# Turning the gathered rows of a routed expert layer's slots, and a block of the layer behind it, on VectorE and through DRAM instead of on TensorE

## The chip, the cores and the metric

One core of a Trainium2 chip runs the whole program. The metric is the time of one execution on the device in microseconds (us). PE is TensorE (PEld its weight loads), DVE is VectorE, ACT is ScalarE, POOL is GpSimd, SP is SyncE; a name like SPq stands for the queue of instructions of that engine.

## The reference

Three stages follow one another on 2304 tokens (4 sequences of 576):

```python
attn_out = _attn_ref(q, k, v, f)                       # causal, with decay; 8 heads of 64
x = attn_out.transpose(0, 2, 1, 3).reshape(2304, 512)

logits = x @ w_gate + modality_bias[modality_id]       # 8 experts
e_idx = np.argmax(logits, axis=1)
gate_w = probs[np.arange(N), e_idx]                    # probs: softmax of logits
for e in range(E):
    mask = e_idx == e
    h = np.maximum(x[mask] @ w1[e], 0.0)               # 512 -> 1024
    out[mask] = gate_w[mask, None] * (h @ w2[e])       # 1024 -> 512

h = out @ w_in                                         # 512 -> 2048
g = np.maximum(0.01 * h, h)
return (g @ w_out).astype(np.float32)                  # 2048 -> 512
```

Each token goes through one expert, and then all tokens through the second layer.

## The kernel before, in words

Matrix products of 32-bit numbers are taken as three products of a high and a low part: ACT casts a value to its high part (names that end in h), DVE subtracts it from the value (names that end in l), and PE multiplies high by high, high by low and low by high.

**Slots.** While attention runs, the tokens are sorted by expert into slots of 128 rows. 18 slots (0 to 17) are always computed; as many more follow as the data need, each behind a test (`go`, L1321). With this data there are 20: slots 0 to 19. The expert, and with it both weight matrices, changes at slots 4, 5 and 10 and nowhere else after slot 0.

A slot's rows are gathered from `xs` by an indirect DMA on POOL's queue (L166) into one of two buffers `xg`, whose last column is the gate. PE turns them, four `tx` transposes of 128x128 (L210) into PSUM, and ACT and DVE make `xh` and `xl` of them (L211, L212). `gemm1` (L222, 24 matmuls of 128x512) gives `h`; `keep` is its relu into `hs` on ACT (L227). `trh` (L1119) turns `hs` on PE, eight transposes, with `hh` and `hl` behind them (L1121, L1122). `gemm2` (L1127, 24 matmuls) sums into `yp`. `yout` scales `yp` with the gate column, which `keepg` has copied to `gc` (L1112), into `ys` on ACT (L1133), and POOL scatters `ys` to the rows of `yd` (L1135). The `ys` buffers are two, in turn.

**A step.** `step(t)` (L1165) lays three slots over one another: gemm1 of slot t, trh and gemm2 of slot t-1, and the turn (`trx`) of slot t+1. Between them stand `split`, which makes the high and low parts of the next slot's weights, w1 (L173, L177) or w2, in pairs, each inside an If that is only taken where the expert changes (L189), and `aside`, small pieces on ACT, DVE and POOL that prepare the second layer's weights or compute slot numbers. The whole runs inside `ordered`: on every engine the instructions stand in the order in which the code emits them, and none overtakes another. So the order of lines in `step` is the order of each queue.

From step 3 on, trx of slot t+1 stands after half of gemm2 and after the first w2 splits:

```python
if t:
    gemm2(t - 1, 0, 4)
...
if t:
    split(t, 1, 0)
    split(t, 1, 1)
if nx and TX <= t < NSTAT - 1:
    trx(t + 1, pmx, "tx")
```

**The end.** After the last slot `tail` (L1142) does the last trh and gemm2. Inside it the first block of the second layer is turned. That layer works on five blocks of up to 512 tokens: block b's rows come from `yd` (`xload`, L994) and are turned by `xts` into `fxh` and `fxl`. Blocks 0 and 1 come in four row DMAs each and are turned by PE, 16 `fx` transposes a block (L1034, L1037, L1038); blocks 2 to 4 come by DMAs that put columns in 32 partitions each and are turned in 32x32 blocks by DVE into `xq` (L1022), with cast and subtraction behind (L1025, L1026). Then `g1` (`u`, L1358) and `g2` (`a`, L1378) follow for 16 pieces of the inner width.

Of the kernel before, what the change touches and what calls it, by code (L numbers as in the profile page):

```python
# [9 lines left out]
F32 = mybir.dt.float32  # L10
# [19 lines left out]
XW = DM + 1  # L30
# [8 lines left out]
NFIX = NTOK % FT  # L39
FIX = NTOK - NFIX  # L40
K1 = 4
T1 = 2
N2 = NS - K1
NSET = 6
SIDE = 2
SP = 2.0
TE = 3
TX = 3
PST = 3
MS = ['PE', 'Activation', 'DVE', 'Pool', 'SP']  # L50
MS2 = ['PE', 'Activation', 'DVE', 'Pool', 'SP']
# [25 lines left out]
def fused(ctx: ExitStack, tc, qk0, qk2, vp, f, mid, wg, mb, w1, w2, w_in, w_out, out):  # L77
# [6 lines left out]
    xs = dr.tile([NTOK, XW], F32, name="xs")  # L84
    agd = dr.tile([4, BH, S], F32, name="agd")
    yd = dr.tile([NTOK, XW], F32, name="yd")


    ident = cp.tile([P, P], F32, name="ident")
# [114 lines left out]
    def flags(i, n):  # L204
        WD.append(nc.values_load(nb[0:1, i:i + 1], engines=(mybir.EngineType.Activation, mybir.EngineType.DVE), min_val=0, max_val=2 ** n - 1))

    def trx(t, pool, tag):
        ps = pool.tile([P, 512], F32, tag=tag, name=f"tx{t}")
        for k in range(NKB):
            nc.tensor.transpose(ps[:, k * P:(k + 1) * P], xg[t % 2][:, k * P:(k + 1) * P], ident)  # L210
        nc.scalar.copy(xh[t % 2], ps)  # L211
        nc.vector.tensor_sub(xl[t % 2], ps, xh[t % 2].bitcast(F32))  # L212
# [12 lines left out]
    def keep(t):  # L225
        hp = Hp.pop(t)
        nc.scalar.activation(WL["hs"], hp.rearrange("p a b -> p (a b)"), AF.Relu)  # L227
# [766 lines left out]
    def xload(b):  # L994
        t0, n = blocks[b]
        r = xp.tile([P, FT // P, XW], F32, tag="xr", name=f"xr{b}")
        if b > 1:
            XR[b] = r.rearrange("p c d -> p (c d)")[:, :4 * n]
            for j in range(4):
                nc.sync.dma_start(XR[b][32 * j:32 * j + 32].rearrange("b (q c) -> b q c", c=P), yd[t0:t0 + n, j * P:(j + 1) * P].rearrange("(q b) c -> b q c", b=32))  # L1000
            if t0 < FIX:
                nc.sync.dma_start(tid[:, t0 // P:(t0 + n) // P].unsqueeze(2), yd[t0:t0 + n, DM:].bitcast(I32).rearrange("(c p) o -> p c o", p=P))
            return
        for i in range(n // P):
            XR[b, i] = r[:, i]
            nc.sync.dma_start(XR[b, i], yd[t0 + i * P:t0 + (i + 1) * P, :])
# [6 lines left out]
    def xts(b, sb, psums, part=None):  # L1013
        t0, n = blocks[b]
        if b not in X:
            xtile(b, sb)
        xh, xl = X[b]
        for i in range(n // P) if part is None else part:
            c = slice(i * P, (i + 1) * P)
            if b > 1:  # L1020
                t = XQ[0].tile([P, 512], F32, tag="xq", name=f"xq{b}_{i}")
                tc.keep_in_program_order(nc.vector.transpose(t.rearrange("p (i k c) -> p i k c", i=4, k=NKB), XR[b][:, i * 512:(i + 1) * 512].rearrange("p (i c k) -> p i k c", i=4, k=NKB)))  # L1022
                t = t.rearrange("p (i k c) -> p k i c", i=4, c=32)
                h, l = (x[:, :, c].rearrange("p k (i c) -> p k i c", c=32) for x in (xh, xl))
                tc.keep_in_program_order(nc.scalar.copy(h, t))  # L1025
                tc.keep_in_program_order(nc.vector.tensor_sub(l, t, h.bitcast(F32)))  # L1026
                continue
            r = XR[b, i]
            nc.gpsimd.tensor_copy(tid[:, t0 // P + i:t0 // P + i + 1], r[:, DM:].bitcast(I32))
            rk = r[:, :DM].rearrange("p (c k) -> p k c", k=NKB)  # L1030
            pool, tag = psums[i % len(psums)]
            ps = pool.tile([P, 512], F32, tag=tag, name=f"fx{b}_{i}")
            for k in range(NKB):
                nc.tensor.transpose(ps[:, k * P:(k + 1) * P], rk[:, k], ident)  # L1034
            yield
            ps = ps.rearrange("p (k c) -> p k c", c=P)
# [54 lines left out]
    with tc.tile_pool(name="rt2", reuse_waits="tile", bufs=1) as rt2, \  # L1091
# [10 lines left out]
        w2l = [mw.tile([P, 2, DM], F32R, name=f"w2l{k}") for k in range(4)]  # L1102
        WL["2h"], WL["2l"] = w2h, w2l
        ysc = []
        hh = mw.tile([P, FF], F32R, name="hh")
        hl = mw.tile([P, FF], F32R, name="hl")
        gc = mw.tile([P, 2], F32, name="gc")

        yp = pmy.tile([P, 512], F32, name="yp")

        def keepg(t):
            nc.scalar.copy(gc[:, t % 2:t % 2 + 1], xg[t % 2][:, DM:DM + 1])  # L1112

        def trh(t):
            for n in range(2):
# [5 lines left out]
                nc.scalar.copy(hh[:, c], ps)  # L1121
                nc.vector.tensor_sub(hl[:, c], ps, hh[:, c].bitcast(F32))  # L1122

        def gemm2(t, k0, k1):
            for k in range(k0, k1):
                for i, (ap, wp) in enumerate(((hh, w2h), (hh, w2l), (hl, w2h))):
                    nc.tensor.matmul(yp, lhsT=ap[:, k * P:(k + 1) * P], rhs=wp[k // 2][:, k % 2, :], start=(k == 0 and i == 0), stop=(k == NFB - 1 and i == 2))  # L1127

        def yout(t):
            m, i = at_slot(oidx, t)  # L1130
            o = m[:, i, :]
            ys = m2.tile([P, XW], F32, tag="ys", name=f"ys{t}")
            nc.scalar.mul(ys[:, :DM], yp, gc[:, t % 2:t % 2 + 1])  # L1133
            nc.gpsimd.tensor_copy(ys[:, DM:].bitcast(I32), o[:, 1:2])
            i = nc.gpsimd.indirect_dma_start(out=yd[:, :], out_offset=bass.IndirectOffsetOnAxis(ap=o[:, 0:1], axis=0), in_=ys, in_offset=None, bounds_check=NTOK - 1, oob_is_err=False)  # L1135
            for o_ in ysc:
                tc.declare_no_dep(i.ins, o_.ins, reason="each token has its own row")
            ysc.append(i)

        LATE = NSTAT - 1  # L1140

        def tail(t):  # L1142
            with ordered(tc, MS4):
                if t >= LATE:
                    yout(t - 1)
                trh(t)
                ps = [(pmx, "tx"), (pma, "h"), (pmb, "h"), (pm0, "th")]
                xs_ = [xts(0, xp0, [p], [i]) for i, p in enumerate(ps)]
                for x in xs_[:3]:
                    next(x)  # L1150
                next(xs_[0])
# [13 lines left out]
        def step(t):  # L1165
            nx = t + 1 < NS
            if t > LATE:
                yout(t - 2)
            if not t:
                with tc.issue_after(st["late"].ins):  # L1170
                    split(t, 1, 0)
                    split(t, 1, 1)
            if t == K1 - 1:
                flags(1, N2)
            keepg(t)
            if t > LATE:
                split(t, 0, 3)
            if t + 2 < NS and t + 2 != K1:
                gather(t + 2)
            if t:  # L1180
                gemm1(t, 0, 2, (pma, pmb)[t % 2], "h")
            aside(t, "load")
            if 0 < t < TE:
                trh(t - 1)
            if nx:
                split(t + 1, 0, 0)
            aside(t, "a1")
            aside(t, "a2")
# [12 lines left out]
            if t:
                gemm1(t, 3, 4, (pma, pmb)[t % 2], "h")
                keep(t)
            if t > NSTAT:
                split(t - 1, 1, 3)
            if nx and t >= NSTAT:
                split(t + 1, 0, 2)
            if nx and 0 < t < LATE:
                split(t + 1, 0, 3)
            if t:  # L1210
                gemm2(t - 1, 0, 4)
            if nx and (0 < t < TX or t >= NSTAT - 1):
                trx(t + 1, pmx, "tx")
            if t:
                split(t, 1, 0)
                split(t, 1, 1)
            if nx and TX <= t < NSTAT - 1:
                trx(t + 1, pmx, "tx")
            if t == K1:
                next(fini, 0)  # L1220
            aside(t, "d")
            if t:
                gemm2(t - 1, 4, 8)
            if t < NSTAT:
                split(t, 1, 2)
            if 0 < t < LATE:
                yout(t - 1)
            if t < NSTAT:
                split(t, 1, 3)

        def finish():
            cnt, full, used = runb, early["full"], early["used"]
# [101 lines left out]
    with tc.tile_pool(name="fx", reuse_waits="tile", bufs=1) as fx, \  # L1334
# [5 lines left out]
         tc.tile_pool(name="pfu", reuse_waits="tile", bufs=3, space=PSUM) as pfu:  # L1340
        for i in range(GS, NSET):
            wset(fx, i)
        XQ.append(xq)
        G = {}
        A = {}
        Y = {}
# [137 lines left out]
```

## Time and profile before

| | |
|---|---|
| time, median of 3 runs | 857.75 us (857.01 to 859.49) |
| the profiled execution, its own time | 857.52 us |
| its span in the trace | 855.8 us |
| granted clock of TensorE, mean | 1.00 |
| PE busy | 847.4 us |
| DVE, ACT, POOL busy | 479.0, 403.4, 133.2 us |
| chain that ended last, by engine | PE 94%, DMA 2%, ACT 2%, DVE 1% |

The span is what the trace covers; the execution's own time is 1.7 us longer. Busy time says how long an engine worked, and not whether it was late for anybody. Matmuls overlap one another, so the time that one costs is the distance between two starts. The chain that ended last is followed from the last instruction back to whatever released each one.

### The profile page before, as it was taken

How to read it: one execution, taken by the hardware profiler on the slowest of the kernel's cores; microseconds unless marked ns; L12 is line 12 of the kernel's file. 1: busy time of each engine (PE TensorE's matmuls, PEld its weight loads, DVE VectorE, ACT ScalarE, POOL GpSimd, SP SyncE). 2: the span in 40 equal slices, each digit the busy share in tenths (PEclk: the TensorE clock that was granted, in tenths of full speed). 3: DMA queues.
4: the chain of work that ended last, by engine and by line, in shares of the span. 5: the costliest groups of instructions: out<-in, count | busy, mean ns of one | idle time of the engine just before them, and what ended most of it. 6: DMA issues, size and time to landing. Idle time of an engine off the chain costs nothing.

```text
span 855.8 us, 14440 instructions
## 1 busy us (share of the span) xinstructions
PE 847.4 (99%) x4724; PEld 700.8 (82%) x4724; DVE 479.0 (56%) x890; ACT 403.4 (47%) x857; POOL 133.2 (16%) x311
## 2 busy tenths in 40 slices
PE   8999999999999999999999999999999999999998
PEld 5888888888887888888888888888888888888887
DVE  7678777778757335233214456686338933473334
ACT  6888878877266355333323344553224422242222
POOL 5102222351146122112121000000000000001111
PEclk9999999999999999999999999999999999999999
DMA  6776787976385254132322231132002300011112
GB/s 210 194 188 178 204 214 201 235 206 207 94 295 190 64 173 137 59 96 75 100 53 66 51 74 50 54 119 75 0 1 74 102 22 1 1 50 50 49 50 74
DMA packets 36579, 92.72 MB, mean 108 GB/s; under 512 B 7017, under 2 KB 12809, under 8 KB 36490
## 3 DMA queue, kind: packets, MB, share of 16 engines
q1 hardware_dynamic: 31834, 76.95, 31.4%
q0 software_dynamic: 4640, 14.71, 5.5%
q8 instruction: 40, 0.66, 0.3%
q14 instruction: 49, 0.40, 0.1%
q10 hardware_dynamic: 16, 0.00, 0.0%
HBM read 131.63 MB, written 14.99 MB: 171 GB/s over the span
## 4 chain that ended last, share of the span: by engine, by line
PE 94%; DMA 2%; ACT 2%; DVE 1%; issue 0%; POOL 0%; SPq 0%; DVEq 0%
PE u L1358 23%; PE a L1378 23%; PE h L222 13%; PE yp L1127 13%; PE pv L547 5%; PE pt L535 3%; PE sc L446 2%; PE th L1119 2%; PE sc L447 2%; DMA aq<-aq 1%; PE xo L571 1%; PE tx L210 1%; ACT p L461 1%; PE pt L525 1%; PE sc L498 1%; PE sc L500 1%
## 5 line engine op out<-in xcount | busy, mean ns | idle before, releaser
L1360 ACT COPY us<-u 128x512 f32<-128x512 f32 (+1 forms) x80 | 43.4, 543 | 169.9 <-PE u L1358 169.5
L1361 DVE SCALAR_TENSOR_TENSOR us<-u,us 128x512 f32<-128x512 f32 (+1 forms) x80 | 50.9, 637 | 125.6 <-ACT us L1360 124.2
L1358 PE MATMUL u<-fxh,wloi 128*128 128x512 f32 (+1 forms) x320 | 117.2, 368 | 0.0
L1358 PE MATMUL u<-fxl,whii 128*128 128x512 f32 (+1 forms) x320 | 117.2, 368 | 0.0
L1358 PE MATMUL u<-fxh,whii 128*128 128x512 f32 (+1 forms) x320 | 116.3, 368 | 0.0
L1378 PE MATMUL a<-whio,gh 128*128 128x512 f32 x280 | 109.3, 391 | 0.0
L1378 PE MATMUL a<-wloo,gh 128*128 128x512 f32 x280 | 109.1, 390 | 0.0
L1378 PE MATMUL a<-whio,gl 128*128 128x512 f32 x280 | 101.9, 389 | 0.0
L461 ACT ACTIVATE p<-sc,nm 128x128 f32<-128x128 f32 (+3 forms) x128 | 66.1, 525 | 24.6 <-DVE nm L456 20.1
L1391 POOL DMA_INDIRECT out<-acc,tid x16 | 16.0, 1001 | 363.9 <-DVE acc L1385 343.7
L1358 PEld LDWEIGHTS u<-fxh,wloi 128*128 128x128 f32 x320 | 60.3, 188 | 10.5
L1358 PEld LDWEIGHTS u<-fxl,whii 128*128 128x128 f32 x320 | 60.3, 188 | 10.3
L1358 PEld LDWEIGHTS u<-fxh,whii 128*128 128x128 f32 x320 | 60.2, 188 | 10.3
L1363 ACT CAST gh<-us 128x512 fp32r<-128x512 f32 (+1 forms) x76 | 44.5, 586 | 49.1 <-DVE us L1361 39.0
L1364 DVE TENSOR_TENSOR gl<-us,gh 128x512 fp32r<-128x512 f32 (+1 forms) x76 | 49.2, 647 | 31.4 <-ACT gh L1363 29.9
L1122 DVE TENSOR_TENSOR hl<-th,hh 128x512 fp32r<-128x512 f32 x40 | 25.8, 686 | 71.9 <-ACT hh L1121 71.9
L456 DVE TENSOR_REDUCE nm<-sc 128x2 f32<-128x256 f32 (+1 forms) x64 | 51.1, 820 | 24.7 <-PE sc L452 18.7
L1127 PE MATMUL yp<-w2h,hh 128*128 128x512 f32 x160 | 64.5, 403 | 0.0
L1127 PE MATMUL yp<-w2h,hl 128*128 128x512 f32 x160 | 62.9, 393 | 0.0
L1127 PE MATMUL yp<-w2l,hh 128*128 128x512 f32 x160 | 62.5, 391 | 0.0
L1378 PEld LDWEIGHTS a<-whio,gl 128*128 128x128 f32 x280 | 52.5, 188 | 11.0
L1378 PEld LDWEIGHTS a<-whio,gh 128*128 128x128 f32 x280 | 52.6, 188 | 10.8 <-ACT gh L1363 0.4
(344 smaller groups left out, 1675.8 us busy)
## 6 DMA issues: line engine op xcount, KB each, us to landing
w1r<-w SPq DMA_DIRECT2D x86, 512.0 KB
w2r<-w SPq DMA_DIRECT2D x82, 512.0 KB
rwi<-w_in SPq DMA_DIRECT2D x16, 512.0 KB
rwo<-w_out SPq DMA_DIRECT2D x16, 512.0 KB
raw<-qk SPq DMA_DIRECT2D x14, 576.0 KB
vt<-vp SPq DMA_DIRECT2D x16, 320.0 KB
bk<-aq SPq DMA_DIRECT2D x14, 288.0 KB
bq<-raw SPq DMA_DIRECT2D x14, 288.0 KB
```

The lines of the kernel that those rows point to most:

```text
L222: nc.tensor.matmul(Hp[t][:, n, :], lhsT=xp[t % 2][:, k * P:(k + 1) * P], rhs=wp[k][:, n * 512:(n + 1) * 512], start=(k == 0 and i == 0), s ...
L456: nc.vector.tensor_reduce(nm, view, axis=AX.X, op=ALU.max, negate=True)
L461: st["exp"] = nc.scalar.activation(pt[:, j, :], view[:, j, :], AF.Exp, bias=nm[:, j:j + 1], scale=1.0, accum_out=sms[g % 3][:, c, j:j + 1])
L547: nc.tensor.matmul(pv_[64 * j:64 * j + 64, q0:w], lhsT=vt[:, j, b, :], rhs=sb[:, j, b, q0:w], start=(b == 0), stop=(b == blocks[-1][0]))
L1122: nc.vector.tensor_sub(hl[:, c], ps, hh[:, c].bitcast(F32))
L1127: nc.tensor.matmul(yp, lhsT=ap[:, k * P:(k + 1) * P], rhs=wp[k // 2][:, k % 2, :], start=(k == 0 and i == 0), stop=(k == NFB - 1 and i == 2))
L1358: nc.tensor.matmul(ps, lhsT=w[:, k * P:(k + 1) * P], rhs=x[:, k, :], start=(i == 0), stop=(i == 3 * NKB - 1))
L1360: nc.scalar.copy(us, ps)
L1361: nc.vector.scalar_tensor_tensor(us, ps, 0.01, us, ALU.mult, ALU.max)
L1363: nc.scalar.copy(gh, us)
L1364: nc.vector.tensor_sub(gl, us, gh.bitcast(F32))
L1378: nc.tensor.matmul(A[b][i], lhsT=x[:, c], rhs=w, start=(first and m == 0), stop=(last and m == 2))
```

## The change

Rows of slots 7 to 17 (counted from 0) go another way. At the end of step t POOL gathers the rows of slot t+3, one step earlier than before. In the next step DVE turns them in 32x32 blocks into a buffer `z`, one of the two `ys` buffers; ACT issues four DMAs that write `z` to a DRAM buffer `xd`, and POOL issues one that reads it back into `xg` with the blocks in their place. Then ACT and DVE make `xh` and `xl` from `xg` in SBUF, without PE.

In all steps trx of slot t+1 now stands ahead of the w2 splits, and from step 4 on `keepg` stands behind trx, with four `gc` columns in place of two.

Block 0 of the second layer is loaded and turned like blocks 2 to 4. Where there is a slot 18, two of its four pieces stand in step 18 behind trx and two at that step's end; otherwise they stand in the tail. The tail's first half of gemm2 takes the terms with `hl` last.

```diff
-TX = 3
+TD = 7
...
+    def turned(t):
+        x = xg[t % 2][:, :DM].rearrange("p (a k x) -> p k a x", a=4, k=NKB)
+        h, l = (i[t % 2].rearrange("p (k a x) -> p k a x", a=4, k=NKB) for i in (xh, xl))
+        nc.scalar.copy(h, x)
+        nc.vector.tensor_sub(l, x, h.bitcast(F32))
+
     def trx(t, pool, tag):
+        if TD <= t < NSTAT:
+            turned(t)
+            return
...
-        if b > 1:
+        if b != 1:
...
+            if b != 1:
+                t = XQ[-1](b, i)
+                pin = tc.keep_in_program_order if b else (lambda x: x)
+                pin(nc.vector.transpose(t.rearrange("p (i k c) -> p i k c", i=4, k=NKB), XR[b][:, i * 512:(i + 1) * 512].rearrange("p (i c k) -> p i k c", i=4, k=NKB)))
                 t = t.rearrange("p (i k c) -> p k i c", i=4, c=32)
                 h, l = (x[:, :, c].rearrange("p k (i c) -> p k i c", c=32) for x in (xh, xl))
-                tc.keep_in_program_order(nc.scalar.copy(h, t))
-                tc.keep_in_program_order(nc.vector.tensor_sub(l, t, h.bitcast(F32)))
+                pin(nc.scalar.copy(h, t))
+                pin(nc.vector.tensor_sub(l, t, h.bitcast(F32)))
...
+        XQ.append(lambda b, i: m2.tile([P, XW], F32, tag="ys", name=f"xq{b}_{i}")[:, :512])
...
-        gc = mw.tile([P, 2], F32, name="gc")
+        gc = mw.tile([P, 4], F32, name="gc")
...
+        def gemm2(t, k0, k1, late=False):
+            terms = [(k, i) for k in range(k0, k1) for i in range(3)]
+            if late:
+                terms = [x for x in terms if x[1] < 2] + [x for x in terms if x[1] == 2]
+            for k, i in terms:
+                ap, wp = ((hh, w2h), (hh, w2l), (hl, w2h))[i]
+                nc.tensor.matmul(yp, lhsT=ap[:, k * P:(k + 1) * P], rhs=wp[k // 2][:, k % 2, :], start=(k == 0 and i == 0), stop=(k == NFB - 1 and i == 2))
...
+        def turn(t):
+            x = xg[t % 2][:, :DM]
+            z = m2.tile([P, XW], F32, tag="ys", name=f"z{t}")[:, :DM]
+            nc.vector.transpose(z.rearrange("p (b k x) -> p b k x", b=4, k=NKB), x.rearrange("p (k b y) -> p b k y", b=4, k=NKB))
+            d = xd[t % 2].rearrange("(b y) (a f) -> a y b f", b=4, a=4)
+            for a in range(4):
+                nc.scalar.dma_start(d[a], z[32 * a:32 * a + 32].rearrange("y (b f) -> y b f", b=4))
...
-                ps = [(pmx, "tx"), (pma, "h"), (pmb, "h"), (pm0, "th")]
-                xs_ = [xts(0, xp0, [p], [i]) for i, p in enumerate(ps)]
-                for x in xs_[:3]:
-                    next(x)
-                next(xs_[0])
                 if t >= NSTAT:
                     split(t, 1, 3, True)
-                gemm2(t, 0, 4)
-                next(xs_[3])
-                for x in xs_[1:]:
-                    next(x)
+                gemm2(t, 0, 4, True)
+                if t < NSTAT:
+                    for i in range(4):
+                        xtr(0, xp0, None, [i])
                 gemm2(t, 4, NFB)
                 yout(t)
...
-            keepg(t)
+            if t <= TD - 3:
+                keepg(t)
             if t > LATE:
                 split(t, 0, 3)
-            if t + 2 < NS and t + 2 != K1:
+            if t + 2 < TD and t + 2 != K1:
                 gather(t + 2)
...
+            if TD <= t + 2 < NSTAT:
+                turn(t + 2)
             if t > NSTAT:
                 split(t - 1, 1, 3)
...
-            if nx and (0 < t < TX or t >= NSTAT - 1):
+            if nx and t:
                 trx(t + 1, pmx, "tx")
+            if t >= TD - 3:
+                if nx:
+                    keepg(t + 1)
+                if t + 3 < NS:
+                    gather(t + 3)
+                if TD <= t + 2 < NSTAT:
+                    nc.gpsimd.dma_start(xg[t % 2][:, :DM], xd[t % 2])
+            if t == NSTAT:
+                for i in range(2):
+                    xtr(0, xp0, None, [i])
             if t:
                 split(t, 1, 0)
                 split(t, 1, 1)
-            if nx and TX <= t < NSTAT - 1:
-                trx(t + 1, pmx, "tx")
             if t == K1
...
+            if t == NSTAT:
+                for i in range(2, 4):
+                    xtr(0, xp0, None, [i])
```

The names in the rows below carry buffer numbers; L190 is the If of the changed kernel, L174 and L178 its weight casts and subtractions, L1036 the `fxh` of block 0, L1148 `ys`, L1353 the test for the next slot.

ACT in step 9, in which slot 10's new weights are split, from `hs` to `xh` of slot 10, before:

```order
L227 ACTIVATE hs_2669<-h9_4681 128x1024
L189 REGISTER_ALU x2
L189 COMPARE_AND_BRANCH
L173 CAST w1h2_111<-w1r2_101 128x1024
L173 CAST w1h3_112<-w1r3_102 128x1024
L189 UNCONDITIONAL_BRANCH x2
L189 REGISTER_ALU x2
L189 COMPARE_AND_BRANCH
L173 CAST w2h0_3241<-w2r0_103 128x1024
L173 CAST w2h1_3242<-w2r1_104 128x1024
L189 UNCONDITIONAL_BRANCH x2
L211 CAST xh0_113<-tx10_4799 128x512
```

and now:

```order
L237 ACTIVATE hs_2671<-h9_4696 128x1024
L1163 DMA xd1_64<-z11_4772 32x4x128 x4
L190 REGISTER_ALU x2
L190 COMPARE_AND_BRANCH
L174 CAST w1h2_113<-w1r2_103 128x1024
L174 CAST w1h3_114<-w1r3_104 128x1024
L190 UNCONDITIONAL_BRANCH x2
L211 CAST xh0_115<-xg0_109 128x512
L1124 COPY gc_3253<-xg0_109 128x1
```

The four DMA issues of slot 11 stand ahead of the second pair of w1 casts, and `xh` stands ahead of the w2 casts.

ACT in step 18, around `xh` of slot 19 and `ys` of slot 17, before:

```order
L211 CAST xh1_2670<-tx19_6269 128x512
L189 COMPARE_AND_BRANCH
L173 CAST w2h0_3241<-w2r0_103 128x1024
L173 CAST w2h1_3242<-w2r1_104 128x1024
L189 UNCONDITIONAL_BRANCH x2
L1321 COMPARE_AND_BRANCH
L1133 ACTIVATE ys17_6302<-yp_3252,gc_3251 128x512
L1112 COPY gc_3251<-xg1_108 128x1
```

and now:

```order
L1124 COPY gc_3253<-xg1_110 128x1
L1036 CAST fxh0_6166<-xq0_0_6305 128x4x128
L1036 CAST fxh0_6166<-xq0_1_6309 128x4x128
L190 COMPARE_AND_BRANCH
L174 CAST w2h0_3243<-w2r0_105 128x1024
L174 CAST w2h1_3244<-w2r1_106 128x1024
L190 UNCONDITIONAL_BRANCH x2
L1036 CAST fxh0_6166<-xq0_2_6332 128x4x128
L1036 CAST fxh0_6166<-xq0_3_6336 128x4x128
L1353 COMPARE_AND_BRANCH
L1148 ACTIVATE ys17_6347<-yp_3254,gc_3253 128x512
```

Four casts of block 0 stand between the gate column of slot 19 and `ys` of slot 17.

DVE in step 4, in which slot 5's new weights are split, before:

```order
L177 TENSOR_TENSOR w1l2_2667<-w1r2_101,w1h2_111 128x1024
L177 TENSOR_TENSOR w1l3_2668<-w1r3_102,w1h3_112 128x1024
L189 UNCONDITIONAL_BRANCH x2
L189 REGISTER_ALU
L189 COMPARE_AND_BRANCH
L177 TENSOR_TENSOR w2l0_3245<-w2r0_103,w2h0_3241 128x1024
L177 TENSOR_TENSOR w2l1_3246<-w2r1_104,w2h1_3242 128x1024
L189 UNCONDITIONAL_BRANCH x2
L212 TENSOR_TENSOR xl1_2671<-tx5_3957,xh1_2670 128x512
```

and now:

```order
L178 TENSOR_TENSOR w1l2_2669<-w1r2_103,w1h2_113 128x1024
L178 TENSOR_TENSOR w1l3_2670<-w1r3_104,w1h3_114 128x1024
L190 UNCONDITIONAL_BRANCH x2
L222 TENSOR_TENSOR xl1_2673<-tx5_3948,xh1_2672 128x512
L190 REGISTER_ALU
L190 COMPARE_AND_BRANCH
L178 TENSOR_TENSOR w2l0_3247<-w2r0_105,w2h0_3243 128x1024
L178 TENSOR_TENSOR w2l1_3248<-w2r1_106,w2h1_3244 128x1024
```

The subtraction that makes `xl` of slot 5 has moved ahead of the w2 pair.

## Rows read from the trace of the kernel before

**Rows 1.** The page's first part: busy time, share and instructions of each engine.

```profile
PE 847.4 (99%) x4724; PEld 700.8 (82%) x4724; DVE 479.0 (56%) x890; ACT 403.4 (47%) x857; POOL 133.2 (16%) x311
```

**Rows 2.** Windows (us, busy, PEclk, DMA share, GB/s): from slot 5's tx, slot 7's.

```profile
257.39:270.98 13.59, 12.65 (x61) 10.15 (x60) 9.77 (x12) 8.53 (x12) 10.86 (x17) 1.00 0.70 226
283.39:295.77 12.38, 12.38 (x61) 10.23 (x60) 2.91 (x5) 3.57 (x6) 2.27 (x3) 1.00 0.30 85
```

**Rows 3.** Timeline of PE, step 9: start, us, engine, line, operation, out<-in, count.

```profile
320.31 0.40 PE L1127 MATMUL yp<-w2h,hl 128*128 128x512 f32 x1
320.54 0.60 PE L210 MATMUL tx<-ident,xg 128*128 128x128 f32 x4
...
321.45 0.40 PE L1127 MATMUL yp<-w2h,hl 128*128 128x512 f32 x1
...
323.73 0.62 PE L222 MATMUL h<-w1h,xh 128*128 128x512 f32 x2
```

**Rows 4.** Timeline of the tail, where block 0's fx transposes stand.

```profile
448.44 1.61 PE L1034 MATMUL fx<-ident,xr 128*128 128x128 f32 x12
...
449.06 1.06 ACT L1121 CAST hh<-th 128x512 fp32r<-128x512 f32 x2
...
449.81 0.47 PE L1127 MATMUL yp<-w2h,hh 128*128 128x512 f32 x1
...
452.90 0.63 PE L1034 MATMUL fx<-ident,xr 128*128 128x128 f32 x4
```

**Rows 5.** ACT's groups by line (busy, mean ns of one | idle before, releaser).

```profile
L1121 ACT CAST hh<-th 128x512 fp32r<-128x512 f32 x40 | 21.5, 589 | 29.5 <-PE th L1119 24.8 <-issue 2.6 <-DVE nb L1257 2.2
```

**Rows 6.** Timeline, end of step 4, DVE and PE, [idle before <-releaser].

```profile
259.58 2.37 DVE L177 TENSOR_TENSOR w2l<-w2r,w2h 128x1024 fp32r<-128x1024 f32 x2
...
262.60 0.74 PE L222 MATMUL h<-w1h,xl 128*128 128x512 f32 x2 [0.94 <-DVE xl L212]
```

**Rows 7.** Timeline of the second layer, block 2 turned by DVE.

```profile
488.59 1.07 DVE L1022 STREAM_TRANSPOSE xq<-xr 128x512 f32<-128x512 f32 x1
...
489.70 0.62 ACT L1025 CAST fxh<-xq 128x512 fp32r<-128x512 f32 x1 [1.75 <-DVE xq L1022]
...
490.96 1.08 DVE L1022 STREAM_TRANSPOSE xq<-xr 128x512 f32<-128x512 f32 x1
```

**Rows 8.** Timeline of step 16: hs on ACT, and the next gemm1 on PE.

```profile
404.66 1.03 ACT L227 ACTIVATE hs<-h 128x1024 f32<-128x1024 f32 x1 [2.14 <-PE h L222]
...
410.41 0.63 PE L222 MATMUL h<-w1h,xh 128*128 128x512 f32 x2
```

**Rows 9.** DMA issues of two lines: ns min/median/max, first and last start us.

```profile
L1006 SPq DMA_DIRECT2D xr<-yd x8: 336/423/430, 422.4 to 461.7; - x8
L347 SPq DMA_DIRECT2D bq<-p x2: 652/744/835, 5.5 to 6.4; - x2
...
L347 ACTq DMA_DIRECT2D bk<-p x1: 1238/1238/1238, 6.3 to 6.3; - x1
```

**Rows 10.** Timeline of step 9: DVE's first w1l pair, ACT's second pair of casts.

```profile
317.20 2.35 DVE L177 TENSOR_TENSOR w1l<-w1r,w1h 128x1024 fp32r<-128x1024 f32 x2
...
318.91 1.99 ACT L173 CAST w1h<-w1r 128x1024 fp32r<-128x1024 f32 x2
```

**Rows 11.** Timeline of step 17: ACT behind an If that is not taken.

```profile
411.52 0.19 ACT L1112 COPY gc<-xg 128x1 f32<-128x1 f32 x1 [0.17 <-ACTq L189]
```

**Rows 12.** Timeline of steps 18 and 19: xl, ys, and gemm2's first matmul.

```profile
433.22 0.69 DVE L212 TENSOR_TENSOR xl<-tx,xh 128x512 fp32r<-128x512 f32 x1 [5.10 <-ACTq L189]
...
435.43 0.69 ACT L1133 ACTIVATE ys<-yp,gc 128x512 f32<-128x512 f32 x1 [2.24 <-PE yp L1127]
...
441.62 0.39 PE L1127 MATMUL yp<-w2h,hh 128*128 128x512 f32 x1
```

**Rows 13.** Timeline of PE at the program's start, the warm-up matmuls.

```profile
1.13 3.17 PE L299 MATMUL wps<-onesb 128*128 128x512 bf16 x7 [1.13 <-DVE onesb L316]
```

**Rows 14.** PE's waits: who it waited for, us in total, times, longest.

```profile
PE wps L299 <- DVE onesb L316: 1.1, 1, 1.1
```

More of the change, by code (lines that the diff above doesn't have):

```diff
@@ L86, in fused @@
     yd = dr.tile([NTOK, XW], F32, name="yd")
+    xd = [dr.tile([P, DM], F32, name=f"xd{i}") for i in range(2)]
     ident = cp.tile([P, P], F32, name="ident")
@@ L1019, in xts @@
             c = slice(i * P, (i + 1) * P)
-            if b > 1:
-                t = XQ[0].tile([P, 512], F32, tag="xq", name=f"xq{b}_{i}")
-                tc.keep_in_program_order(nc.vector.transpose(t.rearrange("p (i k c) -> p i k c", i=4, k=NKB), XR[b][:, i * 512:(i + 1) * 512].rearrange("p (i c k) -> p i k c", i=4, k=NKB)))
+            if b != 1:
+                t = XQ[-1](b, i)
+                pin = tc.keep_in_program_order if b else (lambda x: x)
+                pin(nc.vector.transpose(t.rearrange("p (i k c) -> p i k c", i=4, k=NKB), XR[b][:, i * 512:(i + 1) * 512].rearrange("p (i c k) -> p i k c", i=4, k=NKB)))
                 t = t.rearrange("p (i k c) -> p k i c", i=4, c=32)
                 h, l = (x[:, :, c].rearrange("p k (i c) -> p k i c", c=32) for x in (xh, xl))
-                tc.keep_in_program_order(nc.scalar.copy(h, t))
-                tc.keep_in_program_order(nc.vector.tensor_sub(l, t, h.bitcast(F32)))
+                pin(nc.scalar.copy(h, t))
+                pin(nc.vector.tensor_sub(l, t, h.bitcast(F32)))
                 continue
@@ L1104, in fused @@
         ysc = []
+        XQ.append(lambda b, i: m2.tile([P, XW], F32, tag="ys", name=f"xq{b}_{i}")[:, :512])
         hh = mw.tile([P, FF], F32R, name="hh")
         hl = mw.tile([P, FF], F32R, name="hl")
-        gc = mw.tile([P, 2], F32, name="gc")
+        gc = mw.tile([P, 4], F32, name="gc")
         yp = pmy.tile([P, 512], F32, name="yp")
         def keepg(t):
-            nc.scalar.copy(gc[:, t % 2:t % 2 + 1], xg[t % 2][:, DM:DM + 1])
+            nc.scalar.copy(gc[:, t % 4:t % 4 + 1], xg[t % 2][:, DM:DM + 1])
         def trh(t):
@@ L1122, in trh @@
                 nc.vector.tensor_sub(hl[:, c], ps, hh[:, c].bitcast(F32))
[L1124 to L1127, printed above, removed]
+        def gemm2(t, k0, k1, late=False):
[5 more added lines that the diff above has]
+                nc.tensor.matmul(yp, lhsT=ap[:, k * P:(k + 1) * P], rhs=wp[k // 2][:, k % 2, :], start=(k == 0 and i == 0), stop=(k == NFB - 1 and i == 2))
         def yout(t):
@@ L1132, in yout @@
             ys = m2.tile([P, XW], F32, tag="ys", name=f"ys{t}")
-            nc.scalar.mul(ys[:, :DM], yp, gc[:, t % 2:t % 2 + 1])
+            nc.scalar.mul(ys[:, :DM], yp, gc[:, t % 4:t % 4 + 1])
             nc.gpsimd.tensor_copy(ys[:, DM:].bitcast(I32), o[:, 1:2])
@@ L1342, in fused @@
             wset(fx, i)
-        XQ.append(xq)
+        XQ.append(lambda b, i: xq.tile([P, 512], F32, tag="xq", name=f"xq{b}_{i}"))
         G = {}
```

## The prediction, made before the changed kernel was run

> **What bounds the kernel now.** I read the busy times first: PE is busy 847.4 of 855.8 us and no other engine passes 56% [rows 1]. So an instruction taken off PE shortens the run by its own price, and an instruction given to another engine costs nothing until PE waits for it. I then cut the slots into windows from one group of tx transposes to the next. The reader sees 12.38 us for a steady step, with PE busy all of it, and 13.59 us for the step in which slot 5 takes a new expert [rows 2]. Third, the timeline around the places that the change moves, for how much time lies between a result and the matmul that needs it. Times below are those of the trace; where the change has shifted all engines alike, that shift is left out.
>
> **What leaves PE.** Between the yp matmul at 320.31 and the one at 321.45 lie three matmul intervals and one tx group. Ten intervals from 321.45 to 323.73 give 0.228 us each, so the group costs 1.14 - 0.68 = 0.455 us [rows 3]. Slots 7 to 17 lose it, 11 groups: **-5.0 us**. In their steps nothing else on PE changes.
>
> Block 0's 16 transposes stand in the tail. The first twelve take 448.44 to 449.81, but hh's first half is ready only at 449.06 + 0.59 = 449.65 [rows 4, 5]: PE would have waited anyway, so these twelve give back 0.1, and about 0.15 more because the new order of terms no longer asks for hl so early. The last four, at 452.90, are a whole group, 0.45. Together **-0.7 us**, not sixteen times their price.
>
> **What the new order mends.** In step 4 xl of slot 5 stands behind two w2l subtractions, and PE waits 0.94 us for it [rows 6]; the window is 13.59 - 12.38 = 1.2 us too long [rows 2]. The change puts xl ahead of them. The two subtractions then end about 0.7 us later, and gemm2 reads them only in the next step: **-1.2 us**. POOL now gathers slot 7 before it computes the output indices, so that block and the scatter of slot 3 come later; they are covered while ys of slot 4 isn't waiting for the buffer of slot 3. If that cover went, ACT would be late in step 5 alone.
>
> **What is added, in a steady step.** VectorE gets a transposition of 1.07 us [rows 7], ACT four DMA issues, POOL one more DMA; xh and xl keep their instructions, from SBUF instead of PSUM. ACT queues them as hs, four issues, xh. hs ends at 404.66 + 1.03 = 405.69; gemm1 starts at 410.41, less the tx group 409.96 [rows 8]. With xh at 0.62 [rows 7] there is room for 3.65 us of issues, 0.91 each. No row shows an issue of this shape on ACT. On SP a DMA of 128 pieces takes 0.42; the only issue from ACT took 1.24, for a small copy at the very start [rows 9]. I take 0.46, a little over the SP row, because the shape is nearer to it; the ends are 0.42 and 1.24. At 0.46 a steady step pays nothing. The round trip has two steps: 1.07 for the transposition, 1.8 for the issues, two transfers and a POOL issue stay well under the 24.8 us of two steps [rows 2].
>
> **Step 9, where slot 10 takes a new expert.** Now ACT's issues stand between hs and the second pair of w1 casts, and they wait for z11, which VectorE reaches only after two w1l subtractions: 317.20 + 2.35 + 1.07 = 320.62. Four issues: 322.46. The two casts, 1.99: 324.45. xh, 0.62: 325.07 [rows 7, 10]. PE wants xh at 323.73 - 0.45 = 323.28 [rows 3], so it waits 1.8. VectorE, after the first cast (323.5), does its pair in 2.35 and xl in 0.69: 326.55; PE wants xl four matmuls, 0.92, after its start, at 326.0: 0.5 more. An If that isn't taken costs ACT about 0.17 [rows 11]. **+2.5 us**. With issues of 0.42 it is 2.3, and at 1.24 it is 5.6. Below, if the issues don't hold up ACT at all, it is 0.7.
>
> **Steps 18 and 19, block 0 on VectorE.** The piece of the order that decides: behind xl of slot 19 VectorE does four times transpose, wait for ACT's cast, subtract, and on ACT all four casts stand ahead of ys17 and of hh of slot 18. One piece takes 490.96 - 488.59 = 2.37 us in the second layer, the cast starts 1.11 after its beginning and takes 0.62 [rows 7]. From 433.22 + 0.69 = 433.91 the fourth cast ends at 433.91 + 3 x 2.37 + 1.73 = 442.75. ys takes 0.69, hh 0.59: 444.03 [rows 5, 12]. PE wants hh at 441.62 [rows 12] and so waits 2.4; hl needs as long as xl, 0.69, and is 0.25 late again. Two Ifs and the test for the next slot stand in the run, 0.17 each. **+3.15 us**. The lower end is 0: if VectorE could start the four pieces earlier; the order gives no reason for it. The upper end would add a late load of block 0, but SP issues it at the start of step 18 and the first piece comes at that step's end.
>
> **Sum:** -5.0 - 0.7 - 1.2 + 2.5 + 3.15 = -1.25. The profiled execution took 857.52 us, 0.23 below the median of the runs (857.75): **856.3 us**.
>
> **A rule against it.** A group of four transposes costs PE 0.455 [rows 3], one transposition of a slot's rows costs VectorE 1.07 [rows 7] and then needs the way through DRAM. The Trainium skill (VectorE: DVE Perf Modes, The three transpose paths and Rules for kernel authors) says that VectorE turns 32x32 blocks only, and sends a 128x128 transposition to TensorE where PSUM will do. By the rows the longer way is covered in every turned step, so the sum stays -1.25; by the rule it is the dearer way, and were it on the path the sum would be that of the last rival.
>
> **Rivals.**
> *The stalls do not bite (0.22).* ACT's queue could hand on the DMAs at once, or the chain of block 0 could overlap better than in the second layer, where it shares VectorE with other work. For it: every piece taken from [rows 7] was measured among neighbours. Against: ACT's queue works in order. Without either stall -6.95: 850.6; with half of them 853.5.
>
> *TensorE's clock falls in step 19 (0.12).* PE would stand still for some 3 us; its longest wait for another engine in this trace is 1.1 [rows 14]. At the start, after standing idle, it ran 7 warm-up matmuls in 3.17 us, about 0.42 apart, against 0.228 later [rows 3, 13]: these are the two levels, 1.2 and 2.4 GHz. If the 24 matmuls behind the gap ran at the lower one, 24 x 0.2 = 4.8 us more: 861. The Trainium skill (TensorE: Matmul & The Clock Gate, Why this matters for your kernels) warns that a long enough idle gap between bursts throws the array back to half rate; no row of before has such a gap, so the trace neither bears it out nor denies it.
>
> *ACT's issues are dear (0.11).* This is the one that ends clearly slower. Its place is every turned step, its price is that of one issue, and it decides from 0.91 us. At 1.24, ten steps pay 4 x 0.33 = 1.3, step 9 pays 5.6: -6.9 + 13 + 5.6 + 3.15 = +15, 872 us. For it speaks the single ACT row; against it, that SP at that moment also issued slower than later.
>
> *The longer way comes onto the path (0.05).* The change then doesn't do what it says: PE waits in each turned slot for what VectorE and DRAM deliver. At 1.07 a slot [rows 7], 11 x 1.07 = 11.8 on top of -1.25: 868. Against it speaks the lead of two steps. [...]
>
> **How the numbers follow.** My own case has 0.50. About 0.3%, 2.6 us, is what a measurement of this kernel can tell from no change: faster is below 855.2, slower above 860.3. My case gives faster 0.08, same 0.42; stalls that don't bite, faster 0.22; the clock, same 0.04 and slower 0.08; dear issues, same 0.01 and slower 0.10; the last, slower 0.05. Faster 0.30, same 0.47, slower 0.23. The range goes from 852.0, which leaves out the end without any stall, to 862.0, which takes in the fallen clock and leaves out the dear issues and the longer way.
>
> **What would show it.** PE's tx count falls from 84 to 40, its fx count from 32 to 16. Windows of a steady step shrink from 12.38 to 11.93. In step 9 PE should be idle for 2.5 us, released by xh or xl, and ACT's queue should show four issues between hs and the casts. In step 19 PE should be idle for about 3 us, released by hh, with hl close behind it. The wait for xl in step 4 should be gone. I am wrong if steady windows stay above 12.2, if either gap is under 1 us, or if matmuls behind the gap of step 19 lie 0.4 us apart.

## The result, and the profile after

The changed kernel took 862.28 us (median of 7 runs, 860.15 to 864.66), the kernel before 857.09 (7 runs). The ratio is 1.0057, interval 1.0039 to 1.0075: slower by 0.57%, where 856.3 us and a range of 852 to 862 had been forecast. The profiled execution took 863.93 us, its span is 862.2 us; so the trace read below is 1.65 us longer than the median.

What the change takes off PE is gone: the page's first part, and PE's groups by line.

```profile
PE 844.8 (98%) x4664; PEld 697.7 (81%) x4664; DVE 490.5 (57%) x905; ACT 403.0 (47%) x858; POOL 138.3 (16%) x319
```

```profile
L220 PE MATMUL tx<-ident,xg 128*128 128x128 f32 x40 | 6.0, 272 | 0.0
L1045 PE MATMUL fx<-ident,xr 128*128 128x128 f32 x16 | 2.5, 281 | 0.0
```

PE is busy 2.6 us less than in [rows 1], and the span is 6.4 longer, so it must wait somewhere. PE's waits in the changed kernel (who it waited for, us in total, times, longest):

```profile
PE h L232 <- ACTq L190: 4.7, 1, 4.7
PE h L232 <- ACT xh L211: 2.0, 2, 1.5
PE sc L456 <- DMA aq<-aq: 1.6, 2, 1.1
PE yp L1142 <- ACT hh L1133: 1.3, 1, 1.3
PE wps L309 <- DVE onesb L326: 1.1, 1, 1.1
...
PE h L232 <- DVEq L190: 0.3, 1, 0.3
```

The whole time of a kernel is a poor ruler here: in the traces of this study the attention stage, which the change leaves alone, ended anywhere between 212.1 and 216.9 us. So the table measures the rest in pieces: from the first trh matmul (`th`) of a slot to that of the next, from the last one to the first `u`, and from there to the end. All are differences of starts in PE's timeline. late2, pool2 and pe0 are experiments below.

| stretch | before | after | late2 | pool2 | pe0 |
|---|---|---|---|---|---|
| start to slot 0's th | 212.4 | 213.1 | 216.9 | 214.1 | 213.9 |
| slot 3 to 4 | 13.60 | 12.39 | 12.39 | 12.39 | 12.39 |
| slot 5 to 6 | 12.41 | 12.84 | 12.44 | 12.19 | 11.98 |
| slot 7 to 8 | 12.39 | 11.90 | 11.90 | 11.90 | 11.90 |
| slots 8 to 11, three stretches | 37.14 | 39.67 | 39.94 | 35.68 | 35.68 |
| slots 11 to 16, five stretches | 61.93 | 59.47 | 59.47 | 59.47 | 59.47 |
| slot 18 to 19 | 9.61 | 17.34 | 10.24 | 10.25 | 9.60 |
| slot 19 to the second layer | 8.55 | 7.93 | 8.57 | 8.58 | 8.30 |
| second layer | 399.7 | 399.9 | 399.8 | 399.6 | 399.7 |

The gains are there: 0.48 us in each undisturbed step that turns a slot, 1.21 in step 4, 0.62 in the tail. They are spent in two places. One is the stretch from slot 18 to 19 (+7.7), the other the three stretches from slot 8 to slot 11 (39.67, where pool2 shows 35.68 for the same work). The first of these two numbers scatters: the same instructions took 38.75 to 39.94 in four traces.

**Step 19.** PE's trh of slots 18 and 19, before and then after, and the timeline of ACT and PE between them in the changed kernel:

```profile
437.97 1.04 PE L1119 MATMUL th<-ident,hs 128*128 128x128 f32 x8
447.57 1.03 PE L1119 MATMUL th<-ident,hs 128*128 128x128 f32 x8
```

```profile
437.07 1.04 PE L1131 MATMUL th<-ident,hs 128*128 128x128 f32 x8
...
441.51 0.62 ACT L1036 CAST fxh<-xq 128x512 fp32r<-128x512 f32 x1 [1.75 <-DVE xq L1033]
442.03 0.68 ACT L1148 ACTIVATE ys<-yp,gc 128x512 f32<-128x512 f32 x1
...
442.81 1.22 PE L232 MATMUL h<-w1h,xh 128*128 128x512 f32 x2 [4.71 <-ACTq L190]
442.82 1.07 ACT L1133 CAST hh<-th 128x512 fp32r<-128x512 f32 x2
...
444.68 1.06 PE L232 MATMUL h<-w1h,xl 128*128 128x512 f32 x2
445.54 1.06 PE L232 MATMUL h<-w1h,xh 128*128 128x512 f32 x2
...
448.10 0.63 PE L1142 MATMUL yp<-w2h,hh 128*128 128x512 f32 x1
...
454.41 1.03 PE L1131 MATMUL th<-ident,hs 128*128 128x128 f32 x8
```

PE has finished trh of slot 18 at 438.1 and stands until 442.81. It waits neither for `hh` nor for `ys`, but for an If of line 190 on ACT. Behind the gap two pairs of matmuls lie 0.86 apart, 0.43 a matmul; the undisturbed spacing is 0.23 [rows 3]. The windows of these stretches (us, busy by engine, granted clock, DMA share, GB/s):

```profile
438.00:442.00 4.00, 0.11 (x1) 0.00 (x0) 2.76 (x3) 1.11 (x2) 0.18 (x1) 1.00 0.01 2
442.00:446.00 4.00, 3.19 (x8) 2.54 (x9) 1.98 (x3) 1.79 (x4) 1.03 (x1) 0.50 0.17 66
446.00:450.00 4.00, 4.00 (x13) 3.21 (x12) 0.00 (x0) 1.02 (x1) 0.00 (x0) 0.64 0.00 0
450.00:454.00 4.00, 4.00 (x22) 3.29 (x21) 0.69 (x1) 0.68 (x2) 1.19 (x3) 1.00 0.02 6
```

PE stood still, then the granted clock was 0.50 (1.2 of 2.4 GHz). It came back within the third window: from 448.9 on the matmuls lie 0.23 apart again.

**Step 9.** ACT's and PE's timeline:

```profile
319.29 1.78 ACTq L1163 DMA_DIRECT2D xd<-z  x4
...
321.36 1.99 ACT L174 CAST w1h<-w1r 128x1024 fp32r<-128x1024 f32 x2 [3.26 <-DMA xd<-z]
...
323.26 0.61 ACT L211 CAST xh<-xg 128x512 fp32r<-128x512 f32 x1
...
323.93 0.73 PE L232 MATMUL h<-w1h,xh 128*128 128x512 f32 x2 [1.48 <-ACT xh L211]
```

This is the predicted chain: hs, wait for z11, four issues, two casts, xh. After its 1.48 us, and 0.34 more for xl, the clock was at its lower level here too, which no term of the sum had. Six matmuls lie 0.43 apart:

```profile
326.06 1.06 PE L232 MATMUL h<-w1h,xh 128*128 128x512 f32 x2
326.91 1.06 PE L232 MATMUL h<-w1l,xh 128*128 128x512 f32 x2
```

```profile
324.00:326.00 2.00, 1.66 (x6) 1.09 (x7) 1.85 (x3) 0.69 (x1) 0.00 (x0) 1.00 0.01 4
326.00:328.00 2.00, 2.00 (x6) 1.57 (x5) 0.25 (x1) 1.19 (x2) 1.83 (x3) 0.50 0.65 201
328.00:330.00 2.00, 2.00 (x11) 1.71 (x11) 0.00 (x0) 0.31 (x1) 1.05 (x1) 0.65 0.92 279
```

### The profile page after: what moved, and what is told of

It is laid out like the page before. It is cut to its first block, busy times and chain, and to the rows that moved or that the text cites. A ratio compares the mean times of both kernels' runs of the same rounds, so it can differ in the third digit from the quotient of the medians.

```text
span 862.2 us, 14541 instructions
## 1 busy us (share of the span) xinstructions
PE 844.8 (98%) x4664; PEld 697.7 (81%) x4664; DVE 490.5 (57%) x905; ACT 403.0 (47%) x858; POOL 138.3 (16%) x319
```

## The experiments

Ratios are against the kernel before on the same chip, with 95% intervals.

**late2: block 0's last two pieces later.** The two pieces leave the end of step 18:

```diff
+            if t == NSTAT + 1:
+                for i in range(2, 4):
+                    xtr(0, xp0, None, [i])
             if t:
                 gemm2(t - 1, 0, 4)
...
-            if t == NSTAT:
-                for i in range(2, 4):
-                    xtr(0, xp0, None, [i])
```

(The tail of slot 18 takes them where there is no slot 19.)

> Only pieces 2 and 3 of block 0 move: from the end of step 18 into step 19, behind hs on ACT. Theory Q (the order of ACT's queue): the two casts stood ahead of ys17 and of the If with slot 19's w1 pair, for which PE waited 4.71 us; without them the gap goes, and with it the slow matmuls behind it. From the trh of slot 18 to that of slot 19: 17.34 us before the move, 9.6 after it; the run 862.3 - 7.7 = 854.6 us. Rival D (turning block 0 on VectorE is dear wherever it stands, by its time on VectorE or by its loads): the same pieces now hold up step 19 or the tail, and the run stays over 860 us.

Slot 18 to 19 fell to 10.24 us, the ratio to 0.9997 (0.9983 to 1.0011). So the place of these casts in ACT's queue made the gap, and not VectorE's work as such. Two costs of block 0 stayed. The first two pieces still stand ahead of ys17, and PE waits 0.36 us for the same If, so the stretch is 0.63 above the kernel before. The last two now stand ahead of ACT's entry into the tail, where PE waits 1.93 us for hh in place of 1.31; the 0.62 that the tail had gained is lost again. The time, 857.23, missed the forecast of 854.6: against the changed kernel the median fell by 5.1 us and the trace behind the attention by 6.6, where 7.7 had been forecast.

**warm and warm2: does the gap lower the clock?** Twenty matmuls that nobody needs fill PE's gap in the changed kernel; their sum is read by no one. In warm they read a w1 tile:

```diff
+            if t == NSTAT + 1:
+                wm = pmx.tile([P, 512], F32, tag="tx", name="wm")
+                for i in range(20):
+                    nc.tensor.matmul(wm, lhsT=xh[t % 2][:, :P], rhs=w1h[0][:, :512], start=True, stop=True)
```

> The changed kernel with 20 matmuls more on PE in step 19, ahead of the gap: they multiply data that is there already into a PSUM buffer that nobody reads. 20 x 0.228 = 4.56 us, less than the gap of 4.71. Theory C (the clock falls because PE stands idle in the gap): PE's start behind the gap stays where it is, but the matmuls behind it lie 0.23 apart instead of 0.42; from trh of slot 18 to that of slot 19 17.34 -> 14.3, the run 862.3 - 3.0 = 859.3 us. Rival (the clock falls for some other reason, or the slow matmuls wait for weights): they stay 0.42 apart, and the run stays at 862.

A miss: ratio 1.0142 (1.0127 to 1.0158). The added matmuls themselves waited for an If on ACT (`PE wm L1219 <- ACTq L190: 5.8`) and then ran on the path. warm2 takes `rhs=xh[t % 2]`:

> Again the changed kernel with 20 matmuls more in step 19, but of xh with itself, so that none of them waits for a w1 tile behind an If of ACT (in warm they stood still themselves, 5.8 us). Theory C: PE is busy through the gap, h behind it starts where it did, and its matmuls lie 0.23 apart; from trh of slot 18 to that of slot 19 17.34 -> 14.3 to 14.6, the run 862.3 - 3.0 = 859.3 us. Rival: they stay 0.42 apart, 17.3 us, 862.

Ratio 1.0031 (1.0017 to 1.0045), 859.92 us; slot 18 to 19 took 14.96. PE in warm2, and its windows:

```profile
436.65 4.82 PE L1219 MATMUL wm<-xh 128*128 128x512 f32 x20
441.95 0.74 PE L232 MATMUL h<-w1h,xh 128*128 128x512 f32 x2 [0.48 <-ACTq L190]
442.53 0.63 PE L232 MATMUL h<-w1l,xh 128*128 128x512 f32 x2
442.99 0.63 PE L232 MATMUL h<-w1h,xl 128*128 128x512 f32 x2
...
444.85 0.40 PE L1142 MATMUL yp<-w2h,hh 128*128 128x512 f32 x1
```

```profile
438.00:442.00 4.00, 3.52 (x17) 2.57 (x15) 2.62 (x4) 1.86 (x4) 0.19 (x1) 1.00 0.01 2
442.00:446.00 4.00, 4.00 (x17) 3.25 (x18) 1.29 (x2) 1.99 (x3) 1.04 (x1) 1.00 0.17 66
```

The clock stays at 1.00, the spacing at 0.23. More work on PE made this stretch 17.34 - 14.96 = 2.4 us shorter: standing idle had lowered the clock. (The intervals of the two ratios, 1.0031 and 1.0057, just overlap; the stretch decides.) The lower clock itself cost 2.7 us: from the first matmul behind the gap to the trh of slot 19 it is 454.41 - 442.81 = 11.60 us in the changed kernel and 8.87 in warm2, where that matmul started 0.35 us later behind trh.

**xhfirst, both and mid: xh out from behind the issues.** In xhfirst the cast and subtraction of a turned slot (`turned(t + 1)`) stand right behind `trh(t - 1)`; both adds late2.

> Only the cast and the subtraction of a turned slot (xh, xl) move: from behind half of gemm2 to right behind trh, so ahead of hs, of the four DMA issues and of the second w1 pair. Theory Q: in step 9 xh was late by 1.48 and xl by 0.34 us because they stood behind issues and casts, in step 6 xh by 0.56; all three waits go, and the matmuls behind them run at full rate. Step 9 (trh of slot 8 to that of slot 9) 15.45 -> 11.9 to 12.4, step 6 12.84 -> 11.9, step 10 12.33 -> 11.9; together -4.4 to -4.9, the run 857.5 us. Rival W (the four issues delay the w1 casts themselves, by 2.4 us): PE then waits for the second w1 pair instead, step 9 stays above 13.5, and the run stays at 860 or more.

> The two moves of late2 and xhfirst together. Theory Q: -7.7 - 4.7, so 850 us, 0.83% below the kernel before; PE's only wait over 0.5 us behind the attention is that for hh in the tail, 1.3. Rivals D and W: over 856 us.

Both missed: xhfirst took 866.49 us, 1.0108 (1.0093 to 1.0124), both 860.52, 1.0046 (1.0032 to 1.0059). Slot 8 to 9 took 11.89 as forecast, but slots 8 to 11 together 44.3 in xhfirst against 39.67. Rival W was partly right: PE waited 0.92 us for `w1h` and 0.53 for `w1l`. The larger part had no rival: in the stretches from slot 9 to 11, 15.5 and 16.9 us long, PE waited 1.07 and 1.92 us for `hh` and 1.02 for `hl`, and in the second of them the granted clock fell too. ACT and POOL in xhfirst:

```profile
330.98 0.60 POOL L1243 DMA_DIRECT2D xg<-xd  x1
...
336.05 0.62 ACT L211 CAST xh<-xg 128x512 fp32r<-128x512 f32 x1 [2.96 <-DMA xg<-xd]
...
336.84 1.03 ACT L237 ACTIVATE hs<-h 128x1024 f32<-128x1024 f32 x1 [0.17 <-ACTq L190]
```

xh asked for the reload before it had landed, and hs, the issues and the casts stood behind it. mid therefore puts `turned(t + 1)` behind hs and ahead of `turn(t + 2)`, with late2's move:

> As late2, and the cast and subtraction of a turned slot right behind hs, ahead of the four issues, but not as early as in xhfirst. Theory Q2 (in xhfirst xh stood so early that ACT's whole queue waited for the reload, which landed 5 us after POOL issued it; behind hs it has landed): steps 9, 10 and 11 together, 39.9 us in late2, become 35.7 to 36.5, step 6 12.44 -> 11.9; the run 857.2 - 4.5 = 852.7 us. Rival (the four issues and the wait for z11 hold the second w1 pair back and PE waits for it): steps 9 to 11 stay at 38 or more, the run at 855.5 or more.

Its theory fell too: 856.67 us, 0.9993 (0.9978 to 1.0008), slots 8 to 11 took 41.1. Slot 8 to 9 is right at 11.89, and PE waits a slot later:

```profile
329.22 0.53 PE L1142 MATMUL yp<-w2h,hh 128*128 128x512 f32 x1 [1.00 <-ACT hh L1133]
...
342.33 0.50 PE L1142 MATMUL yp<-w2h,hh 128*128 128x512 f32 x1 [0.64 <-ACT hh L1133]
...
344.09 0.55 PE L1142 MATMUL yp<-w2h,hl 128*128 128x512 f32 x1 [1.03 <-DVE hl L1134]
```

Moving xh only chose which result is late. ACT still waits 1.7 us for the reload at xh and 3.5 for z and the issues ahead of the second w1 pair, and until slot 11 the casts of slot 10's new weights leave it no time to catch up. This is read from mid's trace; the next run tests it.

**pool2: the four issues on POOL.** As late2, with one word changed:

```diff
-                nc.scalar.dma_start(d[a], z[32 * a:32 * a + 32].rearrange("y (b f) -> y b f", b=4))
+                nc.gpsimd.dma_start(d[a], z[32 * a:32 * a + 32].rearrange("y (b f) -> y b f", b=4))
```

> As late2, but POOL issues the four DMAs of a turned slot instead of ACT. Theory Q: ACT's queue no longer waits for z11 nor issues ahead of the second w1 pair; xh of slot 10 is ready at its old place. Steps 9 to 11 together 39.9 -> 35.7 to 36.5, the run 857.2 - 4.5 = 852.7 us. Rival P (an issue costs POOL so much that the gather and the reload behind it come late): POOL's four issues take 2.4 us or more a step by the 0.6 of its reload, xh then waits for the reload in every turned step, steps stay over 12 us, and the run over 857.

Ratio 0.9954 (0.9938 to 0.9971), 853.58 us. Slots 8 to 11 took 35.68, all three stretches at the length of an undisturbed one. (The wait for z and the issues moved together, so this run does not price them apart.) The casts of step 9 no longer wait for z:

```profile
318.30 1.98 ACT L174 CAST w1h<-w1r 128x1024 fp32r<-128x1024 f32 x2
320.18 0.62 ACT L211 CAST xh<-xg 128x512 fp32r<-128x512 f32 x1
```

The price moved to POOL, which has room. The issues by source, in the changed kernel and in pool2 (ns min/median/max, first and last start):

```profile
L1163 ACTq DMA_DIRECT2D xd<-z x44: 309/445/1094, 268.4 to 394.3; - x44
```

```profile
L1163 POOL DMA_DIRECT2D xd<-z x44: 551/562/742, 273.9 to 391.2; - x44
```

**order_only: the kernel before with only the turn ahead of the w2 splits.** Lines `if nx and (0 < t < TX ...)` become `if nx and t:`, and the second place goes.

> The kernel before with one edit: the turn of the next slot stands ahead of the w2 splits in every step, nothing else. Step 4 (trh of slot 3 to that of slot 4) 13.60 -> 12.4, the others as before, the run 857.25 - 1.2 = 856.0 us. Rival: the w2 pair, 0.7 us later, holds up gemm2 of slot 5 in the next step and step 5 grows by as much.

Slot 3 to 4 took 12.39, the other stretches were as before, the one from slot 4 to 5 too, so the rival is out. The ratio, 0.9982 (0.9963 to 1.0001), agrees with -1.2 us and cannot tell it from nothing; the stretch can.

**pe0: pool2's issues, block 0 as before.** Block 0 goes back to row loads and PE's transposes in the tail (`b != 1` becomes `b > 1`, the tail's lines return, its late `hl` terms stay).

> POOL issues the DMAs of the turned slots, as in pool2, and block 0 is loaded and turned as in the kernel before, by PE in the tail, with the terms of hl late. Theory B (ACT takes 2.5 us from the test for slot 20, whose branch it takes, to its first instruction of the tail, and PE waits for that whether or not it has transposes to do; so block 0's transposes are nearly free there and the longer way through VectorE only delays ys17 in step 18): from the trh of slot 18 to that of slot 19 10.25 in pool2 -> 9.6, from there to the first u 8.58 -> 8.4 to 8.6, the run 0.7 us below pool2's: 852.9 us, PE's wait for hh in the tail gone. Rival: block 0's 16 transposes cost PE their own price, 4 x 0.455 = 1.8 us; the tail then takes 10.2 and the run 1 us more than pool2's, 854.7.

850.98 us, ratio 0.9919 (0.9902 to 0.9936), the fastest kernel of the study. Slot 18 to 19 is 9.60 again. In the tail PE fills with transposes the time in which it would wait:

```profile
443.40 0.69 ACT L1148 ACTIVATE ys<-yp,gc 128x512 f32<-128x512 f32 x1 [2.71 <-PE th L1131]
443.45 1.61 PE L1045 MATMUL fx<-ident,xr 128*128 128x128 f32 x12
443.99 1.06 ACT L1133 CAST hh<-th 128x512 fp32r<-128x512 f32 x2
```

The tail took 8.30, against 8.58 in pool2 without these transposes. The rival, 10.2, is out. The time itself was forecast 0.7 us below pool2's; the medians, from two chips, lie 2.6 apart and the traces' spans 1.2. The stretches account for 1.1; what makes up the rest of the medians' distance stays open.

**flat: the price of the transposition.** Blocks 0 and 2 to 4 are read in the order in which their elements lie; their columns so enter in another order, and other numbers come out:

```diff
-XR[b][:, i * 512:(i + 1) * 512].rearrange("p (i c k) -> p i k c", i=4, k=NKB)
+XR[b][:, i * 512:(i + 1) * 512].rearrange("p (i k c) -> p i k c", i=4, k=NKB)
```

> As pool2, but the transposition of blocks 0 and 2 to 4 reads its source in the order in which it lies, as the slots' transposition does, instead of every fourth element; the columns of these blocks so enter in another order, and what is computed is not the reference. Theory S (the step of 16 bytes between the elements read makes it dear): the 14 transpositions fall from 1.09 to 0.70 us each. Rival (the neighbours on VectorE, or the buffers, make it dear): they stay at 1.09. PE is never the waiting one there, so the time stays that of pool2 within 0.7 us, apart from step 18, where two pieces of 0.39 less may take 0.3 off.

VectorE's groups, in flat and then in pool2:

```profile
L1033 DVE STREAM_TRANSPOSE xq<-xr 128x512 f32<-128x512 f32 x14 | 9.6, 700 | 0.6 <-DVEq L190 0.6
```

```profile
L1033 DVE STREAM_TRANSPOSE xq<-xr 128x512 f32<-128x512 f32 x14 | 15.0, 1086 | 0.6 <-DVEq L190 0.6
L1160 DVE STREAM_TRANSPOSE z<-xg 128x512 f32<-128x512 f32 x11 | 7.8, 708 | 2.6 <-DMA xg<-xs,gidx 1.2 <-DVEq L190 1.1 <-POOL gi L607 0.2
```

The step of 16 bytes between the elements read made it 1.09 instead of 0.70. One execution took 851.94 us, 1.6 below pool2's median, more than the 0.7 allowed; a single run does not settle that. Its trace does show where PE had been waiting for these transpositions after all: slot 18 to 19 fell from 10.25 to 9.60, and the tail from 8.58 to 8.26.

## Why the prediction was wrong

**Steps 18 and 19: the step that failed.** The prediction had PE want hh at 441.62 and wait 2.4 us for it. The chain up to ys17 was right: the fourth cast was to end 8.84 us behind xl of slot 19, and did so after 9.12 (442.13 - 433.01). The consumer was wrong: PE waits before it comes to hh. Between trh of slot 18 and gemm2 stand twelve matmuls of gemm1, and the first of them waits for slot 19's second pair of w1 casts. Its If stands in ACT's queue right behind ys17, taken or not. In the order of instructions these rows follow on the last one quoted above for step 18:

```
L1148 ACTIVATE ys17_6347<-yp_3254,gc_3253 128x512
L190 REGISTER_ALU x2
L190 COMPARE_AND_BRANCH
L174 CAST w1h2_113<-w1r2_103 128x1024
L174 CAST w1h3_114<-w1r3_104 128x1024
```

With this data the casts are skipped, and the wait for the end of the If remains: PE stood 4.71 us in place of the forecast 3.15. The prediction's own numbers give it. ys17 would end at 442.75 + 0.69 = 443.44, and the first of the twelve matmuls was due 12 x 0.228 = 2.7 us ahead of the 441.62 at which PE wanted hh, so at 438.9: a wait of 4.6. The twelve matmuls then cover hh, and no wait for it is left. The other thing missing was the clock behind the gap.

**The clock, a rival of 0.12, was the rule.** It was priced for step 19 alone, at 4.8 us if all 24 matmuls ran slowly; 14 did, and the comparison with warm2 puts it at 2.7. Matmuls 0.4 us apart were one of the prediction's own signs of being wrong. The clock fell behind the gap of step 9 as well, and no case held both. Here the traces agree with the Trainium skill (TensorE: Matmul & The Clock Gate, Why this matters for your kernels), which warns of gaps between bursts. They also show that the length of a wait alone does not tell: step 9's waits of 1.48 and 0.34 us were followed by the lower clock, and the single one of 1.93 us in pool2's tail was not; the granted clock is 1.00 there throughout.

**Step 9: right in kind.** Predicted were waits of 1.8 and 0.5 us; they were 1.48 and 0.34; z took 0.70 and not 1.07, which is about that difference. The three stretches lost 39.67 - 35.68 = 4.0 us, 2.2 more than the waits. Of these 2.2 some 1.5 are the clock: six matmuls took 2.56 us in place of 1.4, and the eight transposes behind them 1.17 in place of 0.79.

**Right.** Transposes off PE: 11 x 0.48 = 5.3 us in pe0 (5.0 forecast). Step 4: 1.21 (1.2). The tail: 0.62 (0.7), as long as block 0's last two pieces stand where the change put them. The issue: 0.445 us (0.46 taken, ends 0.42 and 1.24), so a steady step pays nothing; "ACT's issues are dear" is out. "The longer way comes onto the path" is out for the change as made. One small miss: in step 6 one issue took 1.0 us, xh was 0.56 late, and the stretch lost 0.9.

**The sum.** For -5.0, -0.7, -1.2, +2.5 and +3.15 read -5.3, -0.6, -1.2, +4.0 and +7.7 (5.0 for the gap and 2.7 for the clock), with +0.9 for step 6, +0.2 in the second layer and +0.8 in the attention: +6.5, against a span that is 6.4 longer. The medians lie 5.2 apart; the attention, which the change leaves alone, makes 0.8 of the rest. (The rival without stalls has -6.95 where the terms add up to -6.9; nothing hangs on that.)

**The rule against the change.** The Trainium skill (VectorE: DVE Perf Modes, Rules for kernel authors) would keep a 128x128 transposition on TensorE. For the slots the measurement says otherwise: in pe0, which turns eleven of them on VectorE, their stretches are 5.3 us shorter, 0.6% of the run (the rest of its 0.8% is the new order, 1.2 us, and the tail). For block 0 it agrees, with a reservation. From trh of slot 18 to the second layer pe0, on PE, takes 17.91 us and pool2, on VectorE, 18.83; but flat, whose transpositions read their source as it lies, takes 17.87. So what made the way round dearer there is the order in which the source is read, and flat does not compute the reference.

## What to carry to other kernels

Look for the first instruction that a wait can stop on each engine, not the first that reads the result; an If that is skipped still has to be reached in its queue. A DMA issue that waits for another engine's result holds up whatever stands behind it, so give it to an engine with an idle queue rather than move its neighbours. Price an idle gap of the matmul engine with the slower matmuls behind it, and before taking work off it, ask whether that work fills a wait that will be there anyway.

## What the runs showed of the hardware beyond that

- VectorE's 128x512 transposition took 0.70 us with its elements read as they lie and 1.09 with 16 bytes between them.
- The same DMA cost 0.445 us to issue on ACT, with single ones at 1.0 and 1.1, and 0.562 on POOL.
- ACT enters the tail late. In the changed kernel it reached the test for slot 20 at 452.6 and its first instruction behind it at 455.3:

```profile
L1353 ACTq COMPARE_BRANCH  x2: 40/42/45, 441.5 to 452.6; - x2
```

```profile
L1148 ACTq EVENT_SEMAPHORE  x3: 17/38/38, 455.3 to 455.5; - x3
```

  That is the likely cause of PE's wait for hh there; it was read from the trace, and no run moved the branch. In the kernel before, late2, pool2 and pe0 the same way took 2.5 to 2.6 us.
- The reload landed a median 3.2 us after POOL issued it, and once 7.8; whether the weights' loads made that one long was not tried:

```profile
DMA to landing us min/median/max: 3.0/3.2/7.8
```
